# Infini-attention with a Fourier layer: key features turned on VectorE and laid in token order through DRAM, keys projected first, joined value halves in three of five memory sums, features ahead of bf16 parts

## The chip, the cores and the metric

The kernel runs on one core of one Trainium2 chip. The metric is the device time of one execution in microseconds, less is better. The engines are called TensorE (PE), VectorE (DVE), ScalarE (ACT), GpSimd (POOL) and SyncE (SP, which here only issues DMAs).

## The reference

Two independent layers over 2048 tokens of 576 features, whose results are laid side by side. The first (A) is attention in 32 heads of 18 features with a compressive memory: the tokens are taken in four segments of 512; within a segment there is causal softmax attention, and from the segments before comes a linear-attention lookup in a memory `M` (18 x 18 per head) and a normaliser `z`, both with the feature map `phi`.

```python
phi = lambda t: jnp.where(t > 0, t + 1.0, jnp.exp(t))
for s in range(N):                      # N = 4 segments of L = 512
    qs, ks, vs = q[:, :, s], k[:, :, s], v[:, :, s]
    p = _softmax(einsum(qs, ks) * scale + mask);  a_dot = p @ vs
    pq = phi(qs)
    a_mem = (pq @ M) / (pq @ z + 1e-6)
    outs.append(g * a_mem + (1.0 - g) * a_dot)      # g = sigmoid(beta), per head
    pk = phi(ks)
    M = M + pk^T @ vs;  z = z + sum(pk)
# then @ wo
```

The second (B) is the real part of a two-dimensional discrete Fourier transform, as matrix products: `y = Cr @ (x @ Hr^T) - Ci @ (x @ Hi^T)`.

## The kernel before

Float32 accuracy is had by splitting: a float32 operand is held as a rounded half `hi` (float32r) and the rest `lo`, and a product is three matmuls, hi x hi, hi x lo, lo x hi. For the attention scores, queries and keys are held as three bf16 parts. The order of all instructions is written by hand (`manual_schedule`); each engine and each DMA queue takes its instructions in program order. `later(n, fn)` puts work off by n calls of `tick()`. All DMAs of this case are issued by SP, in one queue, and an issue whose data is not ready holds the issues behind it.

There are two parts. **The first part** runs over the four segments `s`. `open_qk(s)` starts the first four of nine 128-wide blocks of the query and key projection in the four banks of the PSUM ring `acc`, each block 14 matmuls of 512 columns (features on partitions, tokens on columns); between them stand the memory sums left from the segment before (`accumulate(3)`). Blocks 0 to 3 are queries, 4 to 7 keys, and block 8 holds the last 64 features of both, queries in its lower half. `project_qk(s, m)` then finishes block m: ACT writes the first bf16 part `p0`, DVE the rest `r`, and `rest()` the second and third part on ACT and POOL, which a DMA stores to DRAM (`qd`, `kd`) one tick later. For queries of segments 1 to 3 `phi` makes features: ACT Relu, ACT Exp, DVE max-add (`e = max(x, 0) + exp(-relu(-x))`), DVE cast to `pq_hi`, POOL rest to `pq_lo`. For keys of segments 0 to 2, ACT keeps the projected block as `KF[m]`. Segment 0 takes the blocks in the order 0 to 8, the others 0 to 3, 8, 4 to 7.

Then `project_v(s, j, ...)` projects the values of 128 tokens at a time, j = 0 to 3, in two halves of 14 matmuls of 288 columns (tokens on partitions). Behind each half comes a step of `lookup(s, j)`: 128 tokens' query features times the memory `md` in five chunks of 8 heads (152 columns, 18 values and one sum per head), three matmuls each. In segments 0 to 2 `k_natural(j)` turns the keys of these tokens into token order: five PE transposes of `KF` into two PSUM banks (`kt`), then `phi` on 576 columns into `kn` hi and lo. `accumulate(j - 1)` adds key features times values of the 128 tokens before to the memory in PSUM (`m_ps`), again five chunks of three matmuls of 152 columns. At the next segment's start `memory()` takes the sums to SBUF, clears what lies off the diagonal blocks on POOL (`affine_select`) and splits them into `md`.

Beside this run: the x of the next segment is loaded and split (`load_x`, `split_x`); `copy_parts(s - 1, n)`, n = 0 to 15, copies the stored bf16 parts within DRAM so that the scores find six parts of each feature; weights are loaded and split (`WQ`, `WK`, `W8`, `WV`), in segment 0 queries' first; segment 3 loads the first Fourier operands (`h_load`, `c_load`, `c_cut`) and attention operands (`stack_load`). DVE's part of a weight split is L120, and L122 and L123 for the tail of 64 features.

**The second part** interleaves the attention of all 32 groups of heads with the Fourier products by a table of costs; the output projection ends the kernel. The change does not touch it.

Of the kernel before, what the change touches and what calls it, by code (L numbers as in the profile page):

```python
# [23 lines left out]
P = 128  # L24
# [4 lines left out]
HEAD0 = [0, 7, 14, 21, 24]  # L29
NPAIR = 108  # L30
# [8 lines left out]
def infini_attention_and_fnet(ctx: ExitStack, tc: tile.TileContext, xT, wqk, w8, wv, wo, beta, xtT, cT, hT, out):  # L39
# [10 lines left out]
    vd = [dram.tile([P, 4, 8, 220], BF16, name=f"vd{s}") for s in range(NSEG)]  # L50
    amd = [dram.tile([4, P, D], F32, name=f"amd{s}") for s in range(NSEG)]
# [15 lines left out]
    ident = const.tile([P, P], F32, name="ident")  # L67
    identity(ident)
# [74 lines left out]
    WQ = weight(wide_tile(L))  # L143
# [10 lines left out]
    WK, WV = weight(wide_tile(L)), weight(wide_tile(D))  # L154
    for k in range(5):
        if k < 2:
            raw = sb.tile([P, L], F32, name="r", tag="r", bufs=3)
            dma(raw, wqk[k, :, L:])
        else:
            raw = load_w(wqk[:, :, L:], L, k)  # L160
        later((1, 1, 1, 1, 2)[k], split_wk, WK, k, raw)
# [10 lines left out]
    later(4, split_w8)  # L172
# [7 lines left out]

    pq_hi = sb.tile([P, 5, L], F32R, name="pq_hi")
    pq_lo = sb.tile([P, 5, L], F32R, name="pq_lo")
    zeros_r(pq_hi[64:, 4, :])
    zeros_r(pq_lo[64:, 4, :])
# [3 lines left out]
    for i in range(2):  # L188
        kn.append(tuple(sk.tile([P, D], F32R, name=f"kn{n}{i}") for n in "hl"))
        a, b = (sk.tile([P, H, 19], F32R, name=f"vn{n}{i}") for n in "hl")  # L190
        pool.memset(a.bitcast(F32)[:, :, DH:], 1.0)
        zeros_r(b[:, :, DH:])
        vn.append((a, b))
# [4 lines left out]
    md_hi, md_lo = (sb.tile([P, 5, 8, 19], F32R, name=f"md{n}") for n in "hl")  # L198
    m_ps = [ps.tile([P, 3, 8, 19], F32, name=f"m{b}", bufs=1) for b in range(2)]

    def phi(pool_, name, src, n, hi, lo):
        e = pool_.tile([P, src.shape[-1]], F32, name=f"{name}e", bufs=2)[:n]
        act.activation(e, src, AF.Relu, scale=-1.0)
        act.activation(e, e, AF.Exp, scale=-1.0)
        dve.scalar_tensor_tensor(e, src, 0.0, e, op0=OP.max, op1=OP.add)
        dve.tensor_copy(hi, e)
        pool.tensor_tensor(lo, e, hi.bitcast(F32), OP.subtract)
# [10 lines left out]
    FIRST, KF = {}, {}  # L218
# [785 lines left out]
```

## Time and profile before

| | |
|---|---|
| time, median of 3 runs | 1009.62 us (1009.13 to 1012.9) |
| the profiled execution | 1009.58 us, its span in the trace 1007.8 us |
| first part, segments 0, 1, 2, 3 | 0 to 57.8, to 117.0, to 176.0, to 228.4 us |
| PE, DVE, ACT, POOL busy, share of the span | 99%, 73%, 71%, 64% |
| DMA | 208.92 MB in 305038 packets, 16 engines 80% busy |

A row of the groups reads: line, engine, operation, output and input tiles with shapes, count, then busy time in us and the mean of one in ns, then the idle time of the engine just before these instructions and who ended it. A row of the timeline or of the chain reads: start in us, duration in us, engine, line, with a count if several are merged. A row of waits reads: who waited for whom, total us, times, the longest. Matmuls overlap in the pipeline, so their durations are longer than the distance from one to the next.

### The profile page before, as it was taken

Reading aid. Unit: us, or ns where it says so; the run is one execution under the profiler, and the core shown is the slowest. Engines: PE = TensorE matmul, PEld = TensorE weight load, DVE = VectorE, ACT = ScalarE, POOL = GpSimd, SP = SyncE. Lnnn points to the kernel's source line nnn. Section 1 sums busy time; section 2 is a strip of 40 time slices with the busy share of each in tenths; the row PEclk is TensorE's granted clock in tenths of the full one; section 3 lists DMA queues with packets and bytes.
Section 4 is the critical chain, followed back from the end, with each engine's and each line's share of the span. In section 5 each row is a group of like instructions: output and inputs, shape, how many; then the busy total and the mean of one; then the engine's idle time right before and its main releaser. Section 6 shows DMA issues by size and latency. Waiting matters only on the chain.

```text
span 1007.8 us, 25664 instructions
## 1 busy us (share of the span) xinstructions
PE 997.1 (99%) x9384; PEld 931.9 (92%) x9384; DVE 735.1 (73%) x1995; ACT 710.8 (71%) x1654; POOL 641.8 (64%) x701
## 2 busy tenths in 40 slices
PE   9999999999999999999999999999999999999998
PEld 8988989899899999999999999999989999999998
DVE  6645647575678777788898778888888889998321
ACT  7656567554777778787878788886767778777243
POOL 2657585776666776766776777767767666768100
PEclk9999999999999999999999999999999999999999
DMA  7538456687467998899999998788999999987565
GB/s 254 179 101 256 183 165 236 206 277 239 128 168 198 224 220 218 195 223 241 222 260 219 239 206 185 175 211 226 226 211 235 232 245 224 257 197 183 132 160 136
DMA packets 305038, 208.92 MB, mean 207 GB/s; under 512 B 206224, under 2 KB 259600, under 8 KB 304912
## 3 DMA queue, kind: packets, MB, share of 16 engines
q1 hardware_dynamic: 304912, 207.29, 80.3%
q8 instruction: 73, 1.20, 0.5%
q14 instruction: 53, 0.43, 0.1%
HBM read 121.32 MB, written 57.93 MB: 178 GB/s over the span
## 4 chain that ended last, share of the span: by engine, by line
PE 83%; DVE 5%; ACT 5%; issue 2%; DMA 2%; POOL 2%; SPq 1%; POOLq 0%; DVEq 0%; ACTq 0%
PE d L518 38%; PE s L678 7%; PE d L80 6%; PE v L80 4%; PE pv L796 4%; PE qk L233 4%; PE d L563 3%; PE d L564 3%; PE d L565 3%; PE pv L797 2%; PE m L326 2%; PE qk L80 2%; PE look L351 1%; PE t L752 1%; PE t L755 1%
## 5 line engine op out<-in xcount | busy, mean ns | idle before, releaser
L684 DVE CUSTOM_DVE_ANT_0 s<-s,causal 128x128 f32<-128x128 f32 (+3 forms) x512 | 250.1, 499 | 80.4 <-PE s L678 73.1
L518 PE MATMUL d<-wide,chi 128*128 128x288 f32 x1408 | 266.3, 306 | 0.8 <-DVE y L587 0.8
L405 POOL TENSOR_TENSOR clo<-craw,chi 128x512 fp32r<-128x512 f32 x158 | 215.0, 1361 | 66.6 <-ACT chi L400 47.0
L518 PEld LDWEIGHTS d<-wide,chi 128*128 128x128 f32 x1408 | 211.8, 189 | 2.7 <-DVE y L587 1.0
L518 PE MATMUL d<-wide,clo 128*128 128x288 f32 x704 | 177.5, 319 | 0.0
L718 POOL TENSOR_TENSOR hl<-pf,hl 128x768 f16<-128x768 f32 x64 | 113.9, 1779 | 42.5 <-ACT hl L714 30.3
L678 PE MATMUL s<-ks,qs 108*128 108x128 bf16 (+3 forms) x512 | 134.0, 304 | 2.7 <-DVE negm L684 2.4
L764 ACT ACTIVATE phi<-t 128x384 f16<-128x384 f32 x128 | 61.7, 482 | 105.8 <-PE t L761 105.7
L707 ACT ACTIVATE pf<-s,nb 128x128 f32<-128x128 f32 (+3 forms) x256 | 128.3, 527 | 6.2
L518 PE MATMUL d<-ab,chi 128*128 128x288 f32 x640 | 126.0, 306 | 0.0
L518 PEld LDWEIGHTS d<-wide,clo 128*128 128x128 f32 x704 | 118.6, 189 | 1.7
L779 DVE TENSOR_TENSOR plo<-pf,phi 128x384 f16<-128x384 f32 (+1 forms) x128 | 115.8, 905 | 0.0
L400 ACT ACTIVATE chi<-craw 128x512 fp32r<-128x512 f32 x160 | 100.1, 626 | 6.5 <-DMA craw<-xtT 4.2
L765 ACT ACTIVATE pf<-t 128x384 f32<-128x384 f32 (+1 forms) x192 | 99.5, 518 | 5.2 <-PE t L752 5.0
L518 PEld LDWEIGHTS d<-ab,chi 128*128 128x128 f32 x640 | 98.5, 189 | 0.6
L714 ACT ACTIVATE hl<-pf 128x768 f16<-128x768 f32 (+1 forms) x128 | 87.4, 730 | 2.0
L518 PE MATMUL d<-ab,clo 128*128 128x288 f32 x320 | 84.8, 314 | 0.0
L563 PE MATMUL d<-wide,chi 128*128 128x288 f32 x256 | 84.0, 328 | 0.0
L564 PE MATMUL d<-wide,chi 128*128 128x288 f32 x256 | 75.6, 295 | 0.0
L565 PE MATMUL d<-wide,clo 128*128 128x288 f32 x256 | 75.5, 295 | 0.0
L718 DVE TENSOR_TENSOR hl<-pf,hl 128x512 f16<-128x512 f32 x64 | 70.3, 1098 | 0.0
L779 POOL TENSOR_TENSOR plo<-pf,phi 128x384 f16<-128x384 f32 x64 | 59.9, 936 | 9.3 <-ACT pf L765 8.2
(198 smaller groups left out, 2526.7 us busy)
## 6 DMA issues: line engine op xcount, KB each, us to landing
craw<-cT SPq DMA_DIRECT2D x128, 256.0 KB
ks<-kd SPq DMA_DIRECT2D x32, 432.0 KB
qs<-qd SPq DMA_DIRECT2D x32, 432.0 KB
craw<-xtT SPq DMA_DIRECT2D x32, 320.0 KB
vd<-vs SPq DMA_DIRECT2D x16, 440.0 KB
vst<-vd SPq DMA_DIRECT2D x32, 220.0 KB
qd<-p SPq DMA_DIRECT2D x16, 384.0 KB
kd<-p SPq DMA_DIRECT2D x16, 384.0 KB
```

Of the source, the lines that this page charges most:

```text
L80: pe.matmul(o, a, b, start=n == 0, stop=n == len(terms) - 1)
L400: act.activation(hi, raw[:, :4], AF.Copy)
L405: engine.tensor_tensor(lo, raw[:, :4], hi.bitcast(F32), OP.subtract)
L518: pe.matmul(o[h], a, b[:, h * 288:h * 288 + 288], start=start, stop=stop)
L563: pe.matmul(o, xh[:, k], wl[k][:, cs], start=k == 0, stop=False)
L564: pe.matmul(o, xh[:, k], wh[k][:, cs], start=False, stop=False)
L565: pe.matmul(o, xl[:, k], wh[k][:, cs], start=False, stop=False)
L678: pe.matmul(o[:, c:c + w], q[:, i * P:w], k[:, :w], start=True, stop=True)
L684: dve.tensor_tensor_reduce(o[:, c:c + w], o[:, c:c + w], CAUSAL[0][:, L - w:], scale=scale, scalar=-LOWEST, op0=OP.add, op1=OP.min, accum_ ...
L707: act.activation(f[:, FIRST_COL[i]:FIRST_COL[i] + w], o[:, c:c + w], AF.Exp, bias=nb[:, i:i + 1], scale=-1.0)
L718: engine.tensor_tensor(hl[:, 1, a:b], f[:, a:b], hl[:, 0, a:b], OP.subtract)
L779: (pool if kind == 2 else dve).tensor_tensor(lo[:, a:b], f[:, a:b], hi[:, a:b], OP.subtract)
```

## The change

Key features are made where keys are projected, as for queries (Relu, Exp, max-add on the block of 512 tokens). DVE's transpose then turns each 32 x 32 square within the block, and stores of 32 partitions each, whose runs are 32 features (128 B), lay it in token order in a DRAM tensor `kx`: four stores for a block, two for block 8, 18 a segment. `key_load(s, j)` fetches 128 tokens' features as rows, and `key_split(j)` makes `kn` hi on ACT and lo on POOL. `k_natural`, its PE transposes, the ACT copies `KF` and the float32 identity go; the two banks go to `acc` (five) and to a third bank of sums.

Keys are projected first (4 to 8, 0 to 3 in segment 0; 8, 4 to 7, 0 to 3 in segments 1 and 2; segment 3 stays as it was), so segment 0 loads and splits WK and W8 ahead of WQ. `vn` holds both halves side by side; in chunks 0, 2 and 4 one matmul multiplies the high key half with both (304 columns, 152 in chunk 4, which now has four heads), and `memory()` adds the two results on DVE. In the lookup, chunk 4 (64 features) holds query hi in the lower and lo in the upper partitions, so that one matmul does its three products. The splitting of the memory comes a tick later.

In `project_qk` the features' Relu stands ahead of `p0`, and their other steps ahead of `rest()`. There are five `p` buffers in place of four. `copy_parts` runs once a block (nine) and the other seven times among the values; `split_x(s + 1, 0)` and `(s + 1, 1)` in segments 1 and 2 stand after the last two blocks instead of among the values.

```diff
+SUMS = ((0, 0, 0, 8, True), (0, 2, 7, 8, False), (1, 0, 14, 8, True), (1, 2, 21, 8, False), (2, 0, 28, 4, True))
...
+    kx = [dram.tile([L, D], F32, name=f"kx{s}") for s in range(NSEG - 1)]
...
-    WQ = weight(wide_tile(L))
+    WK = weight(wide_tile(L))
...
-        raw = load_w(wqk[:, :, :L], L, k)
+        raw = load_w(wqk[:, :, L:], L, k)
         split_x(0, k)
-        split_wk(WQ, k, raw)
+        split_wk(WK, k, raw)
...
-    later(4, split_w8)
+    later(1, split_w8)
+    WQ, WV = weight(wide_tile(L)), weight(wide_tile(D))
+    for k in range(5):
+        if k < 2:
+            raw = sb.tile([P, L], F32, name="r", tag="r", bufs=3)
+            dma(raw, wqk[k, :, :L])
+        else:
+            raw = load_w(wqk[:, :, :L], L, k)
+        later((1, 1, 2, 2, 3)[k], split_wk, WQ, k, raw)
 
...
+    pq_lo = sb.tile([P, 4, L], F32R, name="pq_lo")
...
-    def phi(pool_, name, src, n, hi, lo):
-        e = pool_.tile([P, src.shape[-1]], F32, name=f"{name}e", bufs=2)[:n]
-        act.activation(e, src, AF.Relu, scale=-1.0)
-        act.activation(e, e, AF.Exp, scale=-1.0)
-        dve.scalar_tensor_tensor(e, src, 0.0, e, op0=OP.max, op1=OP.add)
-        dve.tensor_copy(hi, e)
-        pool.tensor_tensor(lo, e, hi.bitcast(F32), OP.subtract)
+    md = sb.tile([P, 5, 2, 8, 19], F32R, name="md")
+    zeros_r(md[64:, 4, 1])
+    m_ps = [ps.tile([P, 3, 8, 19], F32, name=f"m{b}", bufs=1) for b in range(3)]
+
+    def query_features(m, e):
+        if m < 4:
+            dve.tensor_copy(pq_hi[:, m], e)
+            pool.tensor_tensor(pq_lo[:, m], e, pq_hi[:, m].bitcast(F32), OP.subtract)
+        else:
+            dve.tensor_copy(pq_hi[:64, 4], e)
+            pool.tensor_tensor(pq_hi[64:, 4], e, pq_hi[:64, 4].bitcast(F32), OP.subtract)
+
+
+    def key_features(s, m, e):
+        t = sk.tile([P, 16, 32], F32, name="kt", tag="kf", bufs=5)
+        dve.transpose(t.rearrange("p b j -> p (b j)"), e)
+        for a in range(4) if m < 8 else (2, 3):
+            f = (m - 4) * P + 32 * a if m < 8 else L + 32 * (a - 2)
+            later(2, dma, kx[s].rearrange("(b i) f -> i b f", i=32)[:, :, f:f + 32], t[32 * a:32 * a + 32])
+
+    KR = {}
+
+    def key_load(s, j):
+        KR[j] = sk.tile([P, D], F32, name="kr", tag="kf", bufs=5)
+        dma(KR[j], kx[s][j * P:(j + 1) * P])
+
+    def key_split(j):
+        raw = KR.pop(j)
+        hi, lo = kn[j % 2]
+        split(hi, lo, raw, pool)
 
...
+    ORDER = ((4, 5, 6, 7, 8, 0, 1, 2, 3), (8, 4, 5, 6, 7, 0, 1, 2, 3), (8, 4, 5, 6, 7, 0, 1, 2, 3),
+             (0, 1, 2, 3, 8, 4, 5, 6, 7))
...
-            o = ps.tile([P, L], F32, name="qk", tag="acc", bufs=4)
+            o = ps.tile([P, L], F32, name="qk", tag="acc", bufs=5)
             chain(o, qk_terms(s, m))
-        if m >= 4 and s < 3:
-            KF[m] = sk.tile([P, L], F32, name="kf", bufs=5)
-            act.activation(KF[m], o, AF.Copy)
-        p = sb.tile([P, 3, L], BF16, name="p", tag="p", bufs=4)
+        p = sb.tile([P, 3, L], BF16, name="p", tag="p", bufs=5)
         r = sb.tile([P, L], F32, name="r", tag="r", bufs=3)
         p0, p1, p2 = (p[:, 2 - i] if 4 <= m < 8 else p[:, i] for i in range(3))
+        keys, queries = m >= 4 and s < 3, s and (m < 4 or m == 8)
+        if keys or queries:
+            n = P if keys or m < 4 else 64
+            e = (sk if keys else sb).tile([P, L], F32, name="ke" if keys else "qe", bufs=2)[:n]
+            act.activation(e, o[:n], AF.Relu, scale=-1.0)
         act.activation(p0, o, AF.Copy)
         dve.tensor_tensor(r, o, p0, OP.subtract)
-        if s and (m < 4 or m == 8):
-            n = P if m < 4 else 64
-            c = m if m < 4 else 4
-            phi(sb, "q", o[:n], n, pq_hi[:n, c], pq_lo[:n, c])
+        if keys or queries:
+            act.activation(e, e, AF.Exp, scale=-1.0)
+            dve.scalar_tensor_tensor(e, o[:n], 0.0, e, op0=OP.max, op1=OP.add)
+            if queries:
+                query_features(m, e if m < 4 else e[:64])
+            if keys:
+                key_features(s, m, e)
 
...
-    def k_natural(j):
-        o = ps.tile([P, 1024], F32, name="kt", bufs=1)
-        js = slice(j * P, (j + 1) * P)
-        for m in range(4):
-            pe.transpose(o[:, 512 + m * P:512 + (m + 1) * P], KF[4 + m][:, js], ident)
-        pe.transpose(o[:, 384:512], KF[8][:, js], ident)
-        phi(sk, "k", o[:, 448:], P, *kn[j % 2])
-
...
+    def sums(c):
+        b, at, h, heads, both = SUMS[c]
+        rows = P if c < 4 else 64
+        if c < 4:
+            return m_ps[b][:rows, at:at + 1 + both]
+        return m_ps[b][:rows, 0].rearrange("p (k h) e -> p k h e", k=2)
+
+    def accumulate(j, which=(0, 1)):
+        (kh, kl), v = kn[j % 2], vn[j % 2]
+        for n in which:
             for c in range(5):
-                b = c // 3
-                cs = slice(64 + c * P, 64 + (c + 1) * P) if c < 4 else slice(0, 64)
-                o = m_ps[b][:cs.stop - cs.start, c % 3]
-                hs = slice(HEAD0[c], HEAD0[c] + 8)
-                pe.matmul(o, a[:, cs], v[:, hs], start=b not in started, stop=True, skip_group_check=True)
-                started.add(b)
+                b, at, h, heads, both = SUMS[c]
+                o, fs, hs = sums(c), slice(c * P, min(c * P + P, D)), slice(h, h + heads)
+                for lhs, rhs, to in ((((kh, v[:, :, hs], o),) if both else
+                                      ((kh, v[:, 0, hs], o[:, 0]), (kh, v[:, 1, hs], o[:, 0]))) if n == 0 else
+                                     ((kl, v[:, 0, hs], o[:, 0]),)):
+                    pe.matmul(to, lhs[:, fs], rhs, start=b not in started, stop=True, skip_group_check=True)
+                    started.add(b)
 
     def memory():
         mf = sk.tile([P, 5, 8, 19], F32, name="mf")
-        act.activation(mf[:, :3], m_ps[0], AF.Copy)
-        act.activation(mf[:, 3], m_ps[1][:, 0], AF.Copy)
-        act.activation(mf[:64, 4], m_ps[1][:64, 1], AF.Copy)
-        pool.memset(mf[64:, 4], 0.0)
+        pool.memset(mf[:, 4], 0.0)
+        for c in range(5):
+            o = sums(c)
+            f = mf[:o.shape[0], c, 8 - SUMS[c][3]:]
+            act.activation(f, o[:, 0], AF.Copy)
+            if SUMS[c][4]:
+                dve.tensor_tensor(f, f, o[:, 1], OP.add)
...
-        later(4, split, md_hi, md_lo, mf)
+
+        def cut():
+            act.activation(md[:, :4, 0], mf[:, :4], AF.Copy)
+            for up in (0, 64):
+                act.activation(md[up:up + 64, 4, 0], mf[:64, 4], AF.Copy)
+            dve.tensor_tensor(md[:, :4, 1], mf[:, :4], md[:, :4, 0].bitcast(F32), OP.subtract)
+            dve.tensor_tensor(md[:64, 4, 1], mf[:64, 4], md[:64, 4, 0].bitcast(F32), OP.subtract)
+        later(5, cut)
 
...
+        u = chunks(3, 4)
+        u8 = u[:, 1].rearrange("p (k h) e -> p k h e", k=2)
+        pe.matmul(u8, pq_hi[:, 4, js], md[:, 4, :, 4:], start=False, stop=True, skip_group_check=True)
...
-        for n, m in enumerate((0, 1, 2, 3, 8, 4, 5, 6, 7) if s else range(9)):
+        for n, m in enumerate(ORDER[s]):
             project_qk(s, m)
             tick()
             if not more and n >= 5:
                 h_split(0, n - 5)
-            if s and n < 8:
-                copy_parts(s - 1, 2 * n)
-                copy_parts(s - 1, 2 * n + 1)
+            if s:
+                copy_parts(s - 1, n)
             if s in (1, 2) and n >= 4:
                 load_x(s + 1, n - 4)
+            if s in (1, 2) and n >= 7:
+                split_x(s + 1, n - 7)
...
+        if more:
+            key_load(s, 0)
         for j in range(4):
             project_v(s, j, lookup(s, j) if s else iter(()))
             if more:
-                k_natural(j)
+                if j < 3:
+                    key_load(s, j + 1)
+                key_split(j)
             tick()
             for k in ((0, 1), (2, 3), (4,), ())[j] if s == 0 else ():
                 load_x(1, k)
-            if more and j in (1, 2):
+            if s == 0 and j in (1, 2):
                 split_x(s + 1, j - 1)
+            for n in range(9 + 2 * j, min(11 + 2 * j, 16)) if s else ():
+                copy_parts(s - 1, n)
```

More of the change, by code (lines that the diff above doesn't have):

```diff
@@ L66, in infini_attention_and_fnet @@
     identity(ident16)
-    ident = const.tile([P, P], F32, name="ident")
-    identity(ident)
     g = const.tile([P, H], F32, name="g")
@@ L225, in open_qk @@
     def open_qk(s):
[L226 to L228 removed]
+        ms = ORDER[s][:4]
+        for m in ms:
+            FIRST[m] = ps.tile([P, L], F32, name="qk", tag="acc", bufs=5)
+        terms = {m: qk_terms(s, m) for m in ms}
         edges = (0, 6, 14) if s else (0, 3, 6, 9, 14)
         for a, b in zip(edges, edges[1:]):
[L231 removed]
+            for m in ms:
                 for n in range(a, b):
                     pe.matmul(FIRST[m], *terms[m][n], start=n == 0, stop=n == 13)
[L234 to L235 removed]
+                if s and m == ms[0] and a:
+                    accumulate(3, (1,))
             if s and a == 0:
[L237 removed]
+                accumulate(3, (0,))
     def copy_parts(s, n):
```

68 lines of the change are left out of this document (23 added, 45 removed).

## The prediction

> **What bounds the kernel now.** I read the page first, then busy time by stage, TensorE's waits, the chain of waits, and the groups by form.
>
> ```profile
> span 1007.8 us, 25664 instructions
> PE 997.1 (99%) x9384; PEld 931.9 (92%) x9384; DVE 735.1 (73%) x1995; ACT 710.8 (71%) x1654; POOL 641.8 (64%) x701
> PE   9999999999999999999999999999999999999998
> PEclk9999999999999999999999999999999999999999
> DMA  7538456687467998899999998788999999987565
> ```
>
> TensorE (PE) is busy everywhere at full clock, but matmuls overlap, so busy says little by itself. The stages are better. The four rows are segments 0 to 3 of the first part, the only part that the change touches; what follows 228.4 us is the attention with the Fourier product and keeps its code.
>
> ```profile
> 0.00:57.80 57.80, 55.98 (x348) 50.60 (x349) 37.03 (x63) 39.82 (x77) 26.11 (x35) 1.00 0.63 208
> 57.80:117.00 59.20, 58.74 (x379) 53.42 (x379) 31.50 (x70) 37.48 (x81) 38.05 (x39) 1.00 0.56 188
> 117.00:176.00 59.00, 58.81 (x380) 53.46 (x379) 34.59 (x71) 36.83 (x80) 39.66 (x40) 1.00 0.59 194
> 176.00:228.40 52.40, 51.98 (x313) 46.70 (x312) 31.46 (x55) 29.63 (x63) 38.70 (x41) 1.00 0.75 244
> ```
>
> Columns: stretch, its length, busy time of PE, weight loads, VectorE (DVE), ScalarE (ACT), GpSimd (POOL), clock, DMA share, GB/s. DVE, ACT and POOL have a quarter to a half of each segment free. PE's waits in the whole part:
>
> ```profile
> PE kt L223 <- POOL ident L62: 1.4, 1, 1.4
> PE look L351 <- DVE r L259: 0.7, 2, 0.5
> PE v L80 <- DVE vr L306: 0.4, 1, 0.4
> PE kt L284 <- DVE ke L205: 0.2, 1, 0.2
> PE m L326 <- POOL knl L207: 0.2, 1, 0.2
> ```
>
> Only 1.5 us after the warm-up. So the pace at which PE issues is what counts, and the chain gives it where it runs on PE alone:
>
> ```profile
> 106.86 0.63 PE look L351 x6
> 107.49 0.45 PE kt L284 x4
> 107.94 0.11 PE kt L285
> 108.05 1.52 PE m L326 x15
> 109.57 1.88 PE v L80 x14
> 111.45 0.96 PE look L351 x9
> ...
> 117.02 5.50 PE qk L233 x24
> ```
>
> One matmul costs 0.229 us at 512 columns, 0.134 at 288, 0.101 (memory sums) to 0.106 (lookups) at 152: below 288 columns time no longer falls with width. Segment 1 from these prices: 126 x 0.229 + 112 x 0.134 + 60 x 0.106 + 60 x 0.101 + 4 x 0.56 = 58.5 us of its 59.2. The first part is bound by PE's issue; whatever leaves PE there comes off the end, unless a wait takes its place.
>
> **Part by part: what leaves PE.** Transposing key features on PE goes: 12 times 0.45 + 0.11 = 6.7 us. A memory sum falls from 15 matmuls to 12: in chunks 0 and 2 two of 152 columns become one of 304, interpolated between 288 and 512 columns at 0.141 us; in chunk 4 the joined one stays at 152. So 10 x 0.101 + 2 x 0.141 = 1.29 against 1.52, 0.23 saved, 12 times 2.8 us. A lookup falls from 15 to 13: 2 x 0.106, 12 times 2.5 us. Together 12.0 us. The 0.4 us that transposes and sums waited for key features in segment 0 go too.
>
> **What is added elsewhere.**
>
> ```profile
> L831 DVE STREAM_TRANSPOSE ogt<-og 128x128 f32<-128x128 f32 x64 | 15.9, 286 | 0.0
> L259 DVE TENSOR_TENSOR r<-qk,p 128x512 f32<-128x512 f32 x36 | 24.8, 689 | 32.0 <-ACT p L258 30.0 <-POOL p L267 1.6 <-POOL p L270 0.3
> L205 DVE SCALAR_TENSOR_TENSOR qe<-qk,qe 128x512 f32<-128x512 f32 x12 | 8.3, 692 | 16.7 <-ACT qe L204 16.7
> L206 DVE CAST pq_hi<-qe 128x512 fp32r<-128x512 f32 x12 | 5.1, 427 | 0.4
> L203 ACT ACTIVATE qe<-qk 128x512 f32<-128x512 f32 x12 | 7.2, 599 | 10.3 <-DVE r L259 10.3
> L204 ACT ACTIVATE qe<-qe 128x512 f32<-128x512 f32 x12 | 7.6, 633 | 0.4
> L207 POOL TENSOR_TENSOR pq_lo<-qe,pq_hi 128x512 fp32r<-128x512 f32 x12 | 17.3, 1441 | 6.6 <-DVE pq_hi L206 5.8 <-DMA qd<-qd 0.8
> ```
>
> No row shows DVE turning 512 columns; 128 cost 0.29 us, and I take 0.69, the price of other 512-column operations (bounds 0.29 and 4 x 0.29 = 1.15). A key block then asks DVE for r, max-add and turn, 2.1 us, and ACT for at most Relu, Exp and two copies (p0, p1) at about Relu's price, 2.4 us, under the 3.2 us (14 x 0.229) that PE needs for a block: in steady state both keep up. Before, Relu waited for r (10.3 us in L203's row); now it stands ahead of it. The removed ACT copies of keys pay for part. Dividing the fifth lookup chunk, three adds into mf, the later cut and the swapped weight order cost nothing while these engines have that free time; without it they would add under 1 us a segment to whichever engine is late. The fifth accumulation bank comes from the transposes' two banks; a fifth p buffer lets ACT start its copies earlier.
>
> *Segment 0, value weights.* Keys first puts five max-adds and five turns, 6.9 us, on DVE ahead of the last cut of WV.
>
> ```profile
> 13.48 0.68 DVE L122 TENSOR_TENSOR wide<-raw,wide 64x512 fp32r<-64x512 f32 x1
> 21.23 0.69 DVE L259 TENSOR_TENSOR r<-qk,p 128x512 f32<-128x512 f32 x1 [1.18 <-ACT p L258]
> 29.43 0.69 DVE L259 TENSOR_TENSOR r<-qk,p 128x512 f32<-128x512 f32 x1 [1.07 <-ACT p L258]
> 31.59 1.53 DVE L122 TENSOR_TENSOR wide<-raw,wide 64x576 fp32r<-64x576 f32 x1
> 33.15 1.05 DVE L123 TENSOR_TENSOR wide<-raw,wide 64x576 fp32r<-64x576 f32 x1
> 36.71 0.42 PE L80 MATMUL v<-wide,xt 128*128 128x288 f32 x2
> ```
>
> That cut ends at 34.2 now and PE uses it at 36.8. The 6.9 us fill 2.3 us of idle DVE time and move it to 38.8: PE waits 2.0 us. Bounds: 4.3 if no idle time is filled, 0 if the cuts run faster, since L122 took 1.53 us beside POOL and 0.68 at 13.48 with POOL idle. The Trainium skill (SBUF — State Buffer, Who interferes with whom) says that a DVE operation with two SBUF inputs and a GpSimd operation that reads SBUF exclude each other for whole instructions; by that rule the slow price holds, as POOL still cuts p then, and without it the wait would be some 0.9.
>
> *Segments 1 and 2, queries last.* Lookups now need the block projected last. After its end ACT needs Relu, p0, Exp (1.8), DVE max-add and cast (1.1), POOL its low half (1.4): 4.3 us. PE has 1.88 + 0.96 + 1.88 us of work before it, and 0.2 within chunk 3: 4.9. Cover 0.6 us; any lag beyond it is a wait. How large lags were:
>
> ```profile
> 91.78 0.60 ACT L258 ACTIVATE p<-qk 128x512 bf16<-128x512 f32 x1 [2.66 <-DMA kd<-p]
> ```
>
> The last block of segment 1 was taken up 2.7 us late for want of a p buffer. I take 0.5 us a segment (0 to 2.7).
>
> *Key rows through DRAM.* Each segment gets 18 stores of 512 packets of 128 B (9216 packets, 1.18 MB) and four loads. The SP queue issues them, at about
>
> ```profile
> 61.44 0.59 SPq L244 DMA_DIRECT2D kd<-kd  x1
> ```
>
> each: 22 x 0.59 = 13 us a segment for an issuer that waits more than it issues; behind each store stand the stores of p, the copies and the x loads, so the last of these go out some us later than they could. key_load waits for stores two steps old, so it holds SP little; but ACT waits in key_split(0), and behind it stand the value evacuations; PE then waits in accumulate(0). Likewise split_x(s+1, 0 and 1), moved ahead of the values, makes ACT wait if x is late, with the last query block behind it. For the price of a narrow packet:
>
> ```profile
> DMA packets 1179, 0.30 MB, mean 151 GB/s; under 512 B 1179, under 2 KB 1179, under 8 KB 1179
> ## 3 DMA queue, kind: packets, MB, share of 16 engines
> q1 hardware_dynamic: 1179, 0.30, 105.7%
> ```
>
> In these 2 us (280 to 282) only 256 B packets ran: 1.057 x 2 x 16 / 1179 = 28.7 ns each. By bytes (188 GB/s at share 0.56 is 336) a 128 B packet would cost 6 ns. I take 15, half the 256 B one: 9216 x 15 / 16 = 8.6 us, and 3.5 for the loads by bytes. Segment 1 has 0.56 x 59.2 = 33.2 us of DMA time; it then asks for 33.2 + 8.6 + 3.5 = 45 in about 55 (59.2 less its share of the 12.0); at 28.7 ns 53. It fits, but the key stores come bunched in the projections, so loads behind them queue. I take 1 us of waiting a segment (0 to 4).
>
> *Copies moved.* Of the 16 DRAM copies seven move into the value stage. In segments 1 and 2 this makes room for the key stores. In segment 3 they meet the first chunk loads; 0.5 us (0 to 3).
>
> **Sum.** Against the profiled execution of 1009.58 us (span 1007.8 and 1.8 around it; median 1009.62, so no correction): 1009.6 - 12.0 - 0.4 + 2.0 + 2 x (0.5 + 1.0) + 0.5 = 1002.7 us.
>
> **Rivals.** *All covered:* DVE clears WV in time, features and key rows arrive before they are used: 1009.6 - 12.4 = 997.2. For it: the free time of DVE, ACT and POOL, and lags shrink when Relu no longer waits. Against: the 0.6 us margin.
>
> *Gain eaten by queueing:* key rows, x and the first chunks come late, 4 us in each of segments 1 and 2 and 3 at the end, with the 2.0 for WV: 1009.6 - 12.4 + 8 + 3 + 2 = 1010.2. For it: the page's DMA row is at 3 to 8 tenths in this part already. Against: PE runs several us ahead on five banks.
>
> *Slower, narrow stores:* DMA becomes the bound of the first part. It decides once a 128 B store costs over (55 - 33.2 - 3.5) x 16 / 9216 = 0.032 us, 32 ns. At twice the 256 B row, 57 ns, a segment needs 33.2 + 33 + 3.5 = 70 us, 15 more, three times 45: 1009.6 - 12.0 + 45 = 1042.6. For it: no row shows a narrow write to DRAM. Against: 256 B packets stay under 29 ns. The Trainium skill (DMA: Bandwidth & Descriptors, Specifications) states that transfers under 512 B make the engine read, modify and write; that rule would speak for this case. The row above cannot settle it, since those packets go to SBUF.
>
> **How the numbers follow.** A measurement of this kernel can tell about 0.5%, 5 us, from no change. Forecast 0.48 (own range 1000 to 1004.5), all covered 0.24, eaten 0.18, narrow stores 0.10. The first two are faster, 0.72 less 0.01 for the forecast's upper edge: 0.71; the third is the same, 0.19; the fourth slower, 0.10. The range leaves out narrow stores and the edges of the others: 996.5 to 1011.
>
> **What would show it.** Right: segments 1 and 2 near 56 us; no PE rows of kt; 144 rows of memory sums with a 304-column form, 156 of lookups; DVE turns near 0.69 us; PE waiting for WV's cut near 37 us. Wrong: long waits of ACT for kr or x and of PE in the first accumulate (queueing); a DMA share near 1 through all segments (narrow stores); a PE without a wait (covered). If the gain is in the first part but not at the end, the attention part lost it, and my premise that it is bound by PE alone falls.

## The result and the profile after

| | before | after |
|---|---|---|
| median | 1010.58 us (1009.13 to 1012.9) | 1025.08 us (1021.39 to 1026.61, 4 runs) |
| the profiled execution, its span | 1009.58, 1007.8 us | 1021.39, 1019.7 us |
| first part ends at | 228.4 us | 238.3 us |
| second part | 779.4 us | 781.4 us |

The ratio is 1.0136 with a 95% interval of 1.0101 to 1.0171. The change makes the kernel slower by 1.4%; 1002.7 us was forecast, with 996.5 to 1011 as range. The profiled execution is the fastest of the four, so the trace shows 11.9 us of growth and not the 14.5 between the medians. Of these 11.9 us, 9.9 lie in the first part.

The page of the changed kernel, in three of the rows shown of before:

```profile
PE 994.9 (98%) x9264; PEld 927.6 (91%) x9264; DVE 745.6 (73%) x2023; ACT 709.4 (70%) x1665; POOL 639.4 (63%) x698
PE   9899898999999999999999999999999999999998
PEclk9998998999999999999999999999999999999999
```

TensorE has 120 matmuls and 2.2 us of busy time less, but its row and that of its clock, 9 everywhere before, now have 8s in the first part. The stages, segments 0 to 3, in the columns of the prediction:

```profile
0.00:60.00 60.00, 54.64 (x319) 48.11 (x320) 40.65 (x66) 39.64 (x79) 23.07 (x32) 0.97 0.80 237
60.00:125.20 65.20, 59.28 (x339) 53.55 (x339) 33.83 (x75) 36.20 (x83) 36.48 (x39) 0.92 0.67 202
125.20:187.80 62.60, 58.64 (x340) 52.66 (x339) 36.73 (x80) 35.98 (x83) 38.83 (x40) 0.95 0.72 219
187.80:238.30 50.50, 50.50 (x303) 45.48 (x302) 34.62 (x66) 30.98 (x68) 41.00 (x40) 1.00 0.74 251
```

Segments 1 and 2, expected near 56 us, took 65.2 and 62.6 (before 59.2 and 59.0). Segment 3, where no key is turned, took 50.5 against 52.4 and kept its gain. TensorE's waits in the whole execution (who, for whom: total us, times, longest):

```profile
PE look L390 <- DVE pq_hi L204: 5.4, 2, 3.1
PE m L355 <- ACT knh L60: 1.7, 1, 1.7
PE look L390 <- POOL pq_lo L205: 1.5, 2, 0.9
PE m L355 <- POOL knl L61: 1.4, 3, 0.5
PE v L81 <- DVE wide L123: 1.3, 1, 1.3
PE m L355 <- POOL vs L333: 1.2, 1, 1.2
```

Lookups wait for the last query features, sums for the key halves, value matmuls for WV's cut. With the small ones the first part has 13.4 us of waits, against 1.5 before.

The rest is clock and the edges of these waits. The timeline of TensorE in segment 1, and stretches of 1 us of the same time:

```profile
94.27 0.42 PE L81 MATMUL v<-wide,xt 128*128 128x288 f32 x2
97.79 0.71 PE L390 MATMUL look<-md,pq_hi 128*128 128x152 f32 x2 [3.10 <-DVE pq_hi L204]
99.13 0.49 PE L390 MATMUL look<-md,pq_lo 128*128 128x152 f32 x1 [0.63 <-POOL pq_lo L205]
100.45 0.68 PE L81 MATMUL v<-wide,xh 128*128 128x288 f32 x2
101.17 0.68 PE L81 MATMUL v<-wide,xh 128*128 128x288 f32 x2
```

```profile
95.00:96.00 1.00, 0.00 (x0) 0.00 (x0) 0.65 (x2) 1.00 (x3) 0.00 (x0) 1.00 0.94 309
97.00:98.00 1.00, 0.21 (x1) 0.21 (x2) 0.70 (x2) 0.34 (x1) 0.19 (x1) 0.50 0.64 190
102.00:103.00 1.00, 1.00 (x6) 1.00 (x5) 0.93 (x4) 0.41 (x4) 0.00 (x0) 0.50 1.07 413
36.00:44.00 8.00, 6.14 (x33) 5.46 (x32) 4.80 (x9) 6.03 (x13) 5.01 (x4) 0.79 0.63 200
```

In the wait of 3.10 us the granted clock (third number from the right) falls to 0.50 and stays there more than 5 us beyond it. Three value matmuls then take 0.72 us (100.45 to 101.17), 0.24 each instead of 0.134. The last row is segment 0, where no wait was longer than 1.3 us: (1 - 0.79) x 8 x 2 = 3.4 us at half clock. The Trainium skill (TensorE: Matmul & The Clock Gate, Part 1) states that the clock is either full or half, judged over free-running windows of some 3.4 us, and half after an idle window. The stretches here are 3.4 us and its multiples, so the trace agrees; but in segment 0 the clock fell at 38.7 us behind waits of 0.21 and 1.27 us, much shorter than a window, so a threshold of one wholly idle window doesn't hold here.

The balance of the first part: I held the distance from the start of each matmul to the next against its mean in the kernel before, by shape. The work fell by 11.0 us by this count (12.0 were forecast), and beyond it the starts are 20.8 us later than before. The recorded waits grew by 11.9 of these (13.4 against 1.5); 8.9 are left for half clock and the edges of waits. 20.8 - 11.0 = 9.8, against 9.9 measured. Counted by themselves, the matmuls that wait for nobody in the stretches at half clock (20.5 us in all) start 7.9 us late.

Where the waits come from is seen on ScalarE, SyncE and in the chain of waits of segment 1:

```profile
94.28 0.63 ACT L60 ACTIVATE xh<-raw 128x512 fp32r<-128x512 f32 x1 [4.65 <-DMA raw<-xT]
94.82 0.58 ACT L282 ACTIVATE qe<-qk 128x512 f32<-128x512 f32 x1
107.75 0.68 ACT L60 ACTIVATE knh<-kr 128x576 fp32r<-128x576 f32 x1 [4.11 <-DMA kr<-kx]
```

```profile
89.34 0.59 SPq L106 DMA_DIRECT2D raw<-xT  x1
90.04 3.01 SPq L91 DMA_DIRECT2D kx<-kt  x4
93.15 0.88 SPq L91 DMA_DIRECT2D kd<-p  x1
94.07 0.57 SPq L267 DMA_DIRECT2D kd<-kd  x1
94.69 0.63 SPq L106 DMA_DIRECT2D raw<-xT  x1
```

```profile
95.41 5.32 DMA qd<-p
...
100.75 0.41 SPq L106
...
101.20 6.52 DMA kr<-kx
...
107.75 0.69 ACT knh L60
```

The x split stands on ScalarE ahead of the last query block and waits 4.65 us for an x load issued at 89.34; the block's Relu starts at 94.82, and TensorE waits 3.10 us for its features. SP issues with no pause above 0.5 us from 75.9 to 102; the four stores of a key block hold it 2.2 to 3.0 us. The key fetches, behind the last x load, are issued at 101.20 and land 6.5 us later, into DMA engines that are full (share 1.02 to 1.07 from 101 to 104).

### The profile page after: what moved, and what is told of

It reads as the page before. It is cut to its first block, busy times and chain, and to the rows that moved or that the text cites. A ratio compares the mean times of both kernels' runs of the same rounds, so it can differ in the third digit from the quotient of the medians.

```text
span 1019.7 us, 25506 instructions
## 1 busy us (share of the span) xinstructions
PE 994.9 (98%) x9264; PEld 927.6 (91%) x9264; DVE 745.6 (73%) x2023; ACT 709.4 (70%) x1665; POOL 639.4 (63%) x698
## 4 chain that ended last, share of the span: by engine, by line
PE 78%; DVE 6%; DMA 5%; ACT 4%; POOL 3%; issue 3%; SPq 1%; POOLq 0%; DVEq 0%; ACTq 0%
PE d L570 37%; PE s L730 7%; PE d L81 6%; PE pv L848 4%; PE v L81 4%; PE qk L256 4%; PE d L615 2%; PE d L616 2%; PE d L617 2%; PE pv L849 2%; DMA kr<-kx 2%; PE qk L81 2%; POOL p L298 1%; PE m L355 1%; PE t L804 1%
```

## Experiments

All ratios are against the kernel before, beside which each run was timed. Theory Q: key rows and x come late because they queue on SP and in the DMA engines. Theory X: it is the x splits on ScalarE. Theory S: SP's many store issues. Theory K: the way through DRAM is too long in itself. Theory P: TensorE's issue is the bound, each matmul saved is a gain. Theory C: a wait costs more than its length, by the clock. Theory E: Relu behind r makes blocks leave their banks late.

**1. The x splits back among the values** (`split_x(s + 1, 0)` and `(s + 1, 1)` after j = 1 and 2, as before).

> The changed kernel, but the first two x blocks of the next segment are split among the values again (as before the change). In the changed kernel's trace PE waited 6.9 us for the last query block's features in segments 1 and 2, ACT stood 4.7 us for x just ahead of that block, and the granted clock fell to 0.5 after the waits. Theory X (the moved x split is what makes the features late): PE's waits in the lookups fall under 1.5 us, the clock loss after them (some 5 us) goes, time 1025 to about 1014. Theory Q (the DMA side is late as a whole, the SP queue or the DMA engines, and x is only the first to show it): ACT then stands for the key rows instead, PE's waits move to the memory sums, time stays above 1019. Forecast's step (0.5 us a segment for this): no change.

1023.59 us, 1.0136 [1.0121, 1.0151]. The features come in time, and the lateness is at the key rows, 14.7 us in two waits. X falls as the cause of the loss.

**2. Wide stores.** The same 18 stores to another layout of the same size, runs of 2 KB; this leaves out the token order.

```diff
-            later(2, dma, kx[s].rearrange("(b i) f -> i b f", i=32)[:, :, f:f + 32], t[32 * a:32 * a + 32])
+            flat = kx[s].rearrange("t f -> (t f)")[f * L:(f + 32) * L].rearrange("(p c) -> p c", p=32)
+            later(2, dma, flat, t[32 * a:32 * a + 32].rearrange("p b j -> p (b j)"))
```

> The changed kernel with the same 18 stores of 64 KB a segment, but each written as 32 runs of 2 KB: the key rows then hold other numbers, so the memory part of the output is not computed rightly; work and waits are the same. Theory N (the 128 B runs keep the DMA engines busy and delay x and key rows): DMA time per segment falls by some 4 us, x and key rows land 4 us earlier, time 1025 to about 1012. Theory S (SP's issuing is what is late: 18 issues at 0.57 us): no change, within 3 us of 1025. Narrow-store rival of the prediction (57 ns each): already against the trace, would give about 990.

1018.63 us, 1.0083 [1.0064, 1.0102]: the narrow runs were worth 6.5 us in this order, between what the two theories gave.

**3. One wide store a block**: 5 issues in place of 18, the bytes the same, all 128 partitions of a block at once; it leaves out the token order too.

> As the wide stores, but one store of 256 KB a block: 5 issues a segment instead of 18; the key rows hold other numbers, so the memory part of the output is not computed rightly. Theory S (SP's issuing): 13 issues of 0.57 us less, so x and key rows go out 7 us earlier in each of segments 0 to 2, PE's waits for features and key rows nearly vanish with their clock loss, time about 1004 to 1008 where the wide stores alone stay near 1025. Theory N (packets): the same time as the wide stores. What stays in both is WV's wait in segment 0 (2.3 us and 1.7 us of clock).

1008.37 us, 0.999 [0.9973, 1.0007]. Another 10 us go with 13 issues a segment, with the key path otherwise whole. The key stores held SP for 28.5 us in the change, 22.8 in run 2 and 8.3 here. This points to the queue ahead of the key rows, not to the way by itself; the number of issues and the wider store aren't separated. Run 5 keeps the stores as they are.

**4. Only joined sums and lookups, in the kernel before** (chunks 0 and 4, two banks; no key path).

> The kernel before, with the lookup packed to 13 matmuls and two of five memory sums joined (chunks 0 and 4, which two PSUM banks hold); keys are still turned on PE, order and copies as before. Theory P (PE's issue bounds the first part and what leaves it comes off the end, as long as nothing becomes late): 12 x 0.21 for the lookups and 12 x 0.16 for the sums, 4.4 us, so 1010 to about 1005.5. Rival: the three engines' extra steps (adds into mf, three more copies for md) delay the lookups, 1009 to 1011.

1014.97 us, 1.0059 [1.0042, 1.0076]: slower with less work, against Theory P. The projection stages grew from 90.8 to 95.4 us in all. In each of them TensorE waited for a bank until the query features had read it, 3.0 of these 4.6 us:

```profile
PE qk L81 <- DVE qe L205: 3.0, 3, 1.0
```

**5. A new order of issues, the arithmetic untouched**: eight copies at a segment's start, eight among the values; x loaded and split among the values; key rows fetched from the seventh block on.

```diff
+        for n in range(8) if s else ():
+            copy_parts(s - 1, n)
         for n, m in enumerate(ORDER[s]):
...
-            if s:
-                copy_parts(s - 1, n)
-            if s in (1, 2) and n >= 4:
-                load_x(s + 1, n - 4)
-            if s in (1, 2) and n >= 7:
-                split_x(s + 1, n - 7)
+            if more and n >= 6:
+                key_load(s, n - 6)
...
```

> The changed kernel with the same arithmetic, the same stores and the same bytes; only the order of DMA issues differs. Of the 16 copies within DRAM eight are issued at a segment's start and eight among the values (two a step), none beside the key stores; key rows are fetched from the seventh block on; the next x is loaded and split among the values in segments 1 and 2 as in segment 0. Theory Q (key rows and x come late because they stand behind copies, x loads and key stores in SP's queue and in the DMA engines; every wait of TensorE is then followed by a stretch at half clock): waits for key halves and for the last query features in segments 1 and 2 fall from 11 us to under 3 us, half-clock time there from 17 us to under 4 us, and the time from 1021-1025 to 1003-1009 us. Rival K (the way of the key features is too long by itself: turn, stores of 128 B runs, fetch, split; the order of the queue matters little): 1017 us or more, with waits for the key halves over 8 us.

1004.57 us, 0.9949 [0.9935, 0.9963]: 20.5 us less than the change, and faster than before. The waits of Q are gone:

```profile
0.00:59.20 59.20, 54.46 (x319) 47.94 (x319) 40.19 (x67) 39.76 (x79) 22.98 (x32) 0.97 0.81 239
59.20:114.85 55.65, 55.18 (x341) 49.75 (x340) 35.06 (x74) 35.70 (x83) 36.94 (x39) 1.00 0.74 225
114.85:170.45 55.60, 55.10 (x342) 49.80 (x340) 37.72 (x79) 35.94 (x83) 38.42 (x40) 1.00 0.84 248
170.45:221.06 50.61, 50.61 (x304) 45.64 (x304) 33.66 (x66) 31.08 (x68) 40.17 (x40) 1.00 0.79 259
```

Segments 1 and 2 are the 56 us that the prediction wanted, at full clock. The DMA share in them is higher than in the changed kernel, 0.74 and 0.84: the transfers are the same, at other times, and the key stores hold SP as long as before (27.1 us). Q holds, K falls.

**6. Run 5 with pieces moved between VectorE and GpSimd** (value-weight cuts in segment 0, the last query block's low half).

> As the run with the new order of issues, and two pieces taken off VectorE's and GpSimd's late chains: in segment 0 GpSimd cuts the low half of the second and fourth value-weight tiles and of half the tail; in segments 1 to 3 VectorE makes the low half of the last query block instead of GpSimd. Theory Q: the value-weight wait of 2.3 us in segment 0 shrinks to under 1 us, the half-clock stretch of 3.4 us behind it (1.7 us lost) goes, and the wait for the last query features shrinks by 0.7 us a segment; 2.5 to 4 us faster than the run with the new order alone, 999-1005 us. Rival (the late chains end at ScalarE or at the transfer, not at these pieces): within 1 us of the other run.

1005.21 us, 0.995 [0.9929, 0.9971]. Segment 0 fell to 58.3 us, but the second part was 1.3 us longer; no gain is shown.

**7. Run 6 with one wide store a block.**

> As the run with the new order and the shifted pieces, but each key block is stored with one DMA in runs of 2 KB (5 stores in place of 18), which lays the features in another order than the memory sums need; it leaves out the token order. It shows what is left of the stores' price once nothing waits behind them. Theory Q: within 2 us of the run with 18 narrow stores, since the queue then has room. Rival S (the 13 more issues and the narrow runs cost by themselves, wherever they stand): 6 us or more faster than the run with 18 stores, as it was 13 to 17 us faster in the changed kernel's order.

1004.61 us, 0.9945 [0.9923, 0.9967]. The 17 us of runs 2 and 3 are nothing here: a narrow store costs only what waits behind it.

**8, 9. The moves apart**: the copies alone; x loads, splits and key fetches alone.

> The changed kernel with one of the three moves of the new order: of the 16 copies within DRAM eight are issued at a segment's start, eight among the values, none beside the key stores. x loads, x splits and key fetches stay as in the changed kernel. Theory Q1 (the copies are what key stores and x loads stand behind; with them away from there the rest clears in time): 1004-1010 us, waits of TensorE in segments 1 and 2 under 4 us together. Theory Q2 (it is the x loads between the last key stores and the key fetches, and the x splits ahead of the last query block on ScalarE): 1016-1021 us, waits for the last query features still over 3 us.

> The changed kernel with the other two moves: x loaded and split among the values in segments 1 and 2 as in segment 0, key rows fetched from the seventh block on; the copies stay in the projections, one a block. Theory Q2: 1004-1010 us, waits for key halves and last features under 4 us together. Theory Q1: key rows still late behind stores and copies, 1014-1020 us, waits for key halves over 6 us.

1014.55 us, 1.0045 [1.003, 1.006], and 1012.54 us, 1.0017 [1.0, 1.0034]. Neither theory alone: one move gives 10.5 us of the 20.5, the other 12.5. The queue is one, and each takes a part of it away: in the first part of the traces they are worth 9.6 and 8.1 us, and both together in run 5 17.2. The copies alone lose 5.4 us again in the second part.

**10. The wait filled**: run 1 with 44 matmuls whose result nobody reads ahead of the first sums of segments 1 and 2.

> The changed kernel with both x splits back among the values (so that TensorE's wait for key rows is in one place, 14.7 us in two waits), and 44 added matmuls of 304 columns, which multiply x by the value weights into unused columns of the sums' bank, ahead of the first memory sums of segments 1 and 2. They are work for nothing: 44 x 0.14 = 6.2 us a segment. Theory C (a wait costs a second time, because the granted clock falls to half for 3.4 us or a multiple behind it): the added work lies in the wait, the half-clock time of 20.4 us in segments 1 and 2 falls to under 7 us, and the kernel with more work is 7 to 10 us faster than without it: 1013-1017 us against 1023.6. Rival N (the low clock in the records is a mark of the wait and costs nothing beyond it): the same 1023.6 us, or up to 12 us slower where the added work isn't hidden.

1022.07 us, 1.0115 [1.0097, 1.0134]. 12.4 us of added work cost nothing and the clock stayed full in segments 1 and 2, yet only 1.5 us came back, within the intervals. The 7 to 10 us of Theory C were too high for long waits: in run 1 half of the 20.5 us at half clock there (10.1) lay in the waits themselves, and the matmuls behind them started 4.8 us late. Some of that went into new waits, 1.3 us at the lookups of segment 2.

**11. Waits put into the kernel before**: six chains of copies on ScalarE that TensorE has to wait for.

> The kernel before with six added waits of TensorE, three in each of segments 1 and 2 behind the memory sums: a matmul of 64 x 64 x 152, nine copies of 64 x 152 one after the other on ScalarE that start with its result (some 2.5 us), and a matmul that reads the last copy; results go to unused columns. Theory C (a short wait costs again in clock, 3.4 us at half): 6 x (2.5 + 1.7) = 25 us, 1033-1037 us, with half-clock stretches behind the waits. Theory N (a wait costs its own length): 6 x 2.5 = 15 us, 1023-1027 us.

1052.96 us, 1.043 [1.0415, 1.0446]. The chains were longer than meant, since other work stood ahead of them on ScalarE. A row of the waits, then the clock around the first:

```profile
PE m L335 <- ACT gt L339: 26.4, 6, 4.7
...
102.00:103.00 1.00, 0.00 (x0) 0.00 (x0) 0.70 (x1) 0.97 (x3) 1.00 (x2) 1.00 1.03 410
104.00:105.00 1.00, 0.00 (x0) 0.00 (x0) 0.79 (x2) 0.91 (x4) 0.66 (x1) 0.50 1.02 405
108.00:109.00 1.00, 1.00 (x6) 1.00 (x5) 0.00 (x0) 0.00 (x0) 0.00 (x0) 0.50 0.00 0
110.00:111.00 1.00, 1.00 (x9) 1.00 (x9) 0.27 (x1) 0.70 (x2) 0.00 (x0) 0.82 0.00 0
```

Matmul starts are 42.1 us late: 27.0 of recorded waits (26.4 added), 15.1 beyond them, 2.5 us for each. A wait of 4.4 us costs 6.9; that the matmuls behind it run at half clock is in the rows.

**12. The same chains with 22 matmuls in each.**

> The same six chains on ScalarE, and 22 more matmuls of 64 x 64 x 152 (22 x 0.107 = 2.4 us, work for nothing) while TensorE would wait. Theory C: no half-clock stretches, 1023-1027 us, 8 to 10 us less than without the added work. Theory N: the same time as without it, within 2 us.

1054.08 us, 1.0445 [1.0427, 1.0462]. Inconclusive: the added matmuls write where the first copy reads, and waited as well (14.3 us of waits are left, in twelve pieces), and half clock still followed. The longest of these pieces was 1.8 us.

**13. The key path in the new order, without joined sums and lookups.**

> The key path of the change in the new order of issues, without its savings on PE in the sums and lookups: memory sums of 15 matmuls, lookups of 15, md in two tiles, four p buffers, as before. Theory P (TensorE's issue sets the pace once nothing waits, so that each part is worth its matmuls): against the run with the new order (1004.6) 12 x 0.23 + 12 x 0.21 = 5.3 us more, 1009 to 1011, that is no gain over the kernel before. Rival E (the joined sums and lookups save nothing, as the run that joined them alone showed): within 2 us of 1004.6.

1011.27 us, 1.0012 [0.9998, 1.0025]: against run 5 the 5.3 us of matmuls are lost, and 1.4 more; this run also has four `p` buffers. Where little waits, Theory P's prices hold to within these 1.4 us.

**14. Run 4 with Relu ahead of p0.**

```diff
+            act.activation(e, o[:n], AF.Relu, scale=-1.0)
         act.activation(p0, o, AF.Copy)
         dve.tensor_tensor(r, o, p0, OP.subtract)
```

> The run that joined sums and lookups alone in the kernel before, plus the change's order on ScalarE: the features' Relu of a query block ahead of its p0. In that run TensorE waited 1.0 us a segment for a bank that VectorE's query features freed late, the three projection stages took 95.4 us against 90.8, and ScalarE waited 5 us a segment for r ahead of each Relu. Theory E (blocks leave their banks too late because Relu waits for r; with matmuls taken away ahead of them TensorE meets it): the waits for query features go, 1007-1010 us in place of 1015. Rival M (the longer work on the memory, adds and cuts of 64 partitions, delays VectorE and ScalarE at a segment's start): still 1013-1016 us.

1005.11 us, 0.9952 [0.9936, 0.9969]: one instruction moved takes 10 us off run 4, and gives as much as run 5 without the key path. ScalarE in run 4, then here, from p0 of one query block to that of the next:

```profile
70.06 0.58 ACT L258 ACTIVATE p<-qk 128x512 bf16<-128x512 f32 x1
71.44 0.60 ACT L203 ACTIVATE qe<-qk 128x512 f32<-128x512 f32 x1 [0.81 <-DVE r L259]
73.13 0.58 ACT L258 ACTIVATE p<-qk 128x512 bf16<-128x512 f32 x1
```

```profile
70.23 0.58 ACT L265 ACTIVATE p<-qk 128x512 bf16<-128x512 f32 x1
72.71 0.59 ACT L265 ACTIVATE p<-qk 128x512 bf16<-128x512 f32 x1
```

With Relu late a block takes 3.07 us, just under TensorE's 3.2; with Relu first 2.48. I read it so that in run 4 nothing was left to make up the memory's longer work at a segment's start, and TensorE, with less work there, met banks not yet free.

**15. Relu first, alone, in the kernel before.**

> The kernel before with one instruction moved: the Relu of a query block's features stands ahead of p0 on ScalarE. Theory E' (before, TensorE hardly waits: 1.5 us in the first part; the order is worth nothing until matmuls are taken away ahead of the blocks): 1008-1010.5 us, the same as before. Rival F (the order itself is what gained 10 us in the run that joined sums and lookups): 1003 us or less.

1007.68 us, 0.998 [0.9969, 0.9991]: 2 us, so by itself the order is worth little.

**16. Run 5 with Relu late again.**

> The run with the new order (1004.6 us) with one edit of the change undone: the features' Relu stands behind p0 and r again, ahead of Exp, for keys and queries. Theory E (in that order ScalarE waits for VectorE's r at every block with features, and banks come free late): projections of segments 1 and 2 longer by 1 us or more each, the last query features late for the lookups, 1009-1016 us. Rival B (five banks instead of four cover it): 1004-1006 us.

1029.27 us, 1.0192 [1.017, 1.0214]: 24.7 us more than run 5, where Theory E gave 11 at most. ScalarE, from p0 of one key block to that of the next:

```profile
84.87 0.58 ACT L282 ACTIVATE p<-qk 128x512 bf16<-128x512 f32 x1
88.28 0.58 ACT L282 ACTIVATE p<-qk 128x512 bf16<-128x512 f32 x1
```

With Relu late a key block takes 3.41 us, more than TensorE's 3.2, so ScalarE falls behind. In segments 1 and 2 TensorE then waits for query features at each of the first three chunks of the first lookup (11.3 us in twelve waits). Five banks don't cover it.

**17. Run 6 with segment 3's copies as before.**

> The run with the new order, the pieces shifted from VectorE and GpSimd, and segment 3's copies two a block as in the kernel before (no key stores compete there). In the run with the new order the second part took 781.5 us against 779.4, with a wait of 2.1 us for mb behind late loads, and segment 0 took 59.2 us against 57.6. Theory: the wait for mb goes and segment 0 keeps 58.3: 1001-1003.5 us. Rival (the joint between the parts costs by the earlier start itself, wherever the copies stand): 1004-1005.5 us.

1003.75 us, 0.9945 [0.993, 0.996], between the two theories. The wait for mb fell from 1.8 us in run 6 to 0.3.

**18. Run 17 with three edits in segment 0**: gates later, the tail of WV cut a block earlier, low key halves on VectorE.

> The last version with three edits in segment 0: the gates' arithmetic (1.2 us on VectorE) moves from ahead of the value-weight cuts into the values, the tail of the value weights is cut one block earlier, and VectorE instead of GpSimd makes the low half of the key rows. In the last version segment 0 had 3.4 us of waits of TensorE and 1.6 us of half clock behind them, the segments after it 1.1 us. Theory: both go, 4 to 5 us: 998.5-1001 us. Rival (the waits move to the next late operand of segment 0): 1002.5-1004.5 us.

1002.80 us, 0.9931 [0.9911, 0.995], the fastest. The rival was right: the wait for WV is gone, and one of 2.8 us for key rows has taken its place, with 3.4 us of half clock behind it.

```profile
PE m L355 <- ACT knh L60: 2.8, 1, 2.8
```

Its interval overlaps that of run 14, so that the key path adds anything to Relu first and joined sums isn't shown.

## Why the prediction was wrong

Right were: the work that leaves TensorE (a memory sum of 12 matmuls in 1.28 us, 0.23 less a lookup, no transposes), the turn (0.71 us for 0.69) and the price of a 128 B packet (13 ns in the median of the packet records, for 15). "Narrow stores" as a bound by bandwidth is out. WV's last cut came out by luck (it ends at 39.18 for 38.8, with 1.9 us of waits for 2.0, by other parts: see the end). The reading that below 288 columns time no longer falls with width was too strong, as its own rows have 0.134 us at 288 and 0.101 at 152; no term used it.

```profile
L213 DVE STREAM_TRANSPOSE kt<-ke 128x512 f32<-128x512 f32 x15 | 10.7, 710 | 0.4
117.44 1.28 PE m L355 x12
```

These steps failed:

- **Key rows, "1 us of waiting a segment"**, and **last query features, "0.5 us a segment"**. Together segments 1 and 2 waited 5.9 and 4.0 us. The prediction named both ways, SP's queue and the x splits ahead of the last block, but priced them by averages: 13 us of issues in a segment, 45 of 55 us of DMA time. In the 25 us that count, key stores, copies and x loads came together and had SP and the DMA engines full. Runs 5, 8 and 9 show that it was the place of the issues: in run 5, with the same stores, copies and loads at other times, the waits of segments 1 and 2 are 1.0 us in all. The rival "gain eaten by queueing" had the mechanism and too small a price.
- **No term for the clock.** 7.9 us by the starts of matmuls. The prediction saw full clock everywhere and took a wait to cost its length.
- **Segment 0 had one wait only.** The sums there waited 1.6 us more, for GpSimd's vs and knl. Half clock came behind the waits for WV and cost another 1.4 us.
- **Relu ahead of p0 at nothing.** The prediction read ScalarE's 10.3 us of waits for r and gave the move no term. Runs 14 and 16 make it the largest single effect: 10 us in one surrounding, 25 in the other, and 2 alone (run 15). It is no reason for the loss. That the change would have been slower still without it follows from run 16 by likeness only; it wasn't run in the change's own order.
- **The premise that the second part keeps its time**: it took 2.0 us more. A wait of 1.1 us for mb is new; it belongs to the term for the moved copies ("0.5 us"), since run 17, with segment 3's copies as before, nearly loses it; the waits for negm are as before, 2.5 us for 2.4. The other 0.9 us stay open.

The 20.5 us between the change and run 5 are settled as queueing, with the clock behind its waits. In the two traces segments 1 and 2 differ by 16.6 us: 8.9 of waits, 6.6 of matmuls late at half clock, the rest at the edges of waits. What waits of this length would cost if the clock stayed full isn't settled, as run 12 was inconclusive.

## What to carry to other kernels

When work moves off the bound engine onto DMA, draw the queue in order of time: what is issued in the few microseconds ahead of the late operand, not what a stage holds in the mean. A wait in a kernel that runs at full clock can cost more than its length. And before taking work off a bound engine, look at the pace of the engines that empty its banks: where theirs is equal, the gain is theirs to give, and one instruction moved ahead of a wait can be worth more than the matmuls saved.

## What was not expected of the hardware

- Half clock behind waits of 1.3 us and less, for 3.4 us; behind six waits of 4.4 us, 2.5 us lost each. It doesn't always follow: run 4 has 7.7 us of waits in the first part, none above 1.3 us, and full clock throughout. What decides isn't shown.
- A store holds its issuer for long. The 54 key stores and the 12 fetches, min, median and max in ns:

```profile
L91 SPq DMA_DIRECT2D kx<-kt x54: 302/490/1406, 20.0 to 157.0; - x54
L222 SPq DMA_DIRECT2D kr<-kx x12: 320/504/635, 42.2 to 180.6; - x12
```

The 54 wide stores of run 2, with a sixteenth of the runs, still held it 422 ns in the median.

The Trainium skill (Perfetto Trace Analysis, DMA Instruction — HWDGE) states that the issuing sequencer is held while descriptors are made, and that the recorded time is this and not the transfer. The rows agree: a fetch is recorded with 0.64 us at most, and the one issued at 101.20 landed 6.5 us later.
- The two subtractions of WV's tail, 1.53 and 1.05 us before, took 0.74 and 0.76 here:

```profile
37.65 0.74 DVE L123 TENSOR_TENSOR wide<-raw,wide 64x576 fp32r<-64x576 f32 x1
38.42 0.76 DVE L124 TENSOR_TENSOR wide<-raw,wide 64x576 fp32r<-64x576 f32 x1
...
36.53 1.16 POOL L298 TENSOR_TENSOR p<-r,p 128x512 bf16<-128x512 f32 x1 [1.96 <-ACT p L297]
38.68 1.52 POOL L298 TENSOR_TENSOR p<-r,p 128x512 bf16<-128x512 f32 x1 [0.99 <-ACT p L297]
```

GpSimd's instruction ended 0.04 us after the first began, and its next, begun during the second, took 0.36 us longer than the one ahead of it. The rule that the prediction drew on (the Trainium skill, SBUF — State Buffer, Who interferes with whom) has whichever comes first make the other wait for a whole instruction. The rows agree in direction: the one that came later grew, by 0.36 us where 0.50 of VectorE's were left. The prediction's slow price was wrong here, since GpSimd came later. The cuts were 1.08 us faster and still ended 0.4 later, so VectorE filled some 1.5 us less idle time than forecast, and the two errors nearly cancelled.
